# Score weights for the product with the values: 64x64 tiles, or 64x32 tiles four side by side

## The chip, the cores and the metric

The kernel runs on one core of a Trainium2 chip. The metric is the device time of one execution in microseconds (us); the time before is the median of three executions.

## What is computed

The reference has two stages. The first is a linear attention with decay, for 4 batches, 8 heads, 768 steps and a head width of 48. For each step t of each head,

```python
y[t] = r[t] @ (state + outer(u * k[t], v[t]))
state = w[t][:, None] * state + outer(k[t], v[t])
```

The second is a gated feed-forward layer on the result x of 3072 rows by 384: `(sigmoid(x @ w_gate) * (x @ w_val)) @ w_out`, with an inner width of 1536. All of it is in 32-bit floats.

## The kernel before

The attention is done by chunks of 128 steps: 6 chunks in each of 4 batches, 24 in all, numbered q. In the names, `pin` holds a chunk's decays, k and r with the head width on the partitions (two heads side by side, at partitions 0 to 47 and 64 to 111, so that p runs over 4 pairs of heads and o over the two of a pair); `tok` holds r, k and v with the steps on the partitions. A chunk is cut in two halves of 64 steps (`HALVES`), and goes through these functions:

- `prep_k`, `prep_r`, `fade` (lines 315 to 342) on VectorE (DVE) scale k, r and the state by running products of the decay.
- `turn_k` (352) transposes k on TensorE (PE), `take_k` copies it out on ScalarE (ACT), and `sums` (389 to 398) multiplies it with the values. Its weights are 64x64 for o = 0 and 64x48 for o = 1, and 48 value columns stream through. `middle` and `keep` (406, 410) update the state.
- `scores` (358 to 380) multiplies k and r to 64x64 blocks of scores (line 370, 48x64 weights, 64 columns stream) and r with the state into the result (line 377, 48x64 weights, 48 columns stream). The two heads and the two halves make four tiles of the array, used in turn.
- `mask` (383) copies the scores, with later steps set to zero, into the tile `at`, one DVE instruction for each o.
- `mix` (412 to 420) multiplies the masked scores, as weights, with the 48 columns of the values, and adds to the result. For half s the weights lie on the partitions of that half and the result goes to the partitions of the same half: the two tiles used are the two on the diagonal. The two heads of a pair write to two different PSUM banks, and `turn` swaps which half goes with which head. There are 2 x 4 x 2 = 16 calls in a chunk; in 32-bit floats each call is two weight loads and two products in the trace.
- `take_y` (424) on DVE adds the bonus term (made on GpSimd, POOL), `turn_x` (429) transposes the result on PE, and `take_x`, `rest_x` (438, 442) split it in a high and a low part.

The feed-forward layer works in groups of chunks of the four batches: `gate` and `value` (both line 450, tiles `pg` and `pu`, nine 128x128 products each), `sigmoid` and `hidden...` on ACT and DVE (461 to 476), `down` (485, tile `po`).

Two pieces of code set the order. Chunks 0 to 11, and the feed-forward groups that are ready by then, are ordered ahead of time by a planner (`Plan`, lines 141 to 187), which plays through costs written in the code; `mix` has a cost of 0.5 there (line 541), and the weights' own preparation (`w_...`, lines 242 to 266) is in the same plan. Chunks 12 to 23 follow a fixed pattern (`steps`, lines 583 to 603, and the loop at 607 to 625): each chunk's attention is spread over three feed-forward steps of the group before it. There `mix` comes right after a `gate`, and a `value` right after `mix`:

```python
gate(*a)
sigmoid(*a)
trio[i][0]()    # i == 1: mix, take_y twice, bonus1, bonus2 of the next chunk
value(*a)
```

Of the kernel before, what the change touches and what calls it, by code (L numbers as in the profile page):

```python
# [1 line left out]

# [16 lines left out]
B, H, S, D = 4, 8, 768, 48  # L19
# [5 lines left out]
NP = H // 2  # L25
# [12 lines left out]
HC = C // 2  # L38
HALVES = [slice(0, HC), slice(HC, C)]
# [151 lines left out]
def tile_kernel(ctx: ExitStack, tc: tile.TileContext, dec: bass.AP, tok: bass.AP, wts: bass.AP, u: bass.AP, out: bass.AP):  # L191
    nc = tc.nc
# [76 lines left out]
    pin, tk, eg, bon, kT, att, ready, mid, bank, x = {}, {}, {}, {}, {}, {}, {}, {}, {}, {}  # L269
# [115 lines left out]
    def values(q, p, o, half):  # L385
        h = 2 * p + o
        return tk[q][half, 2 * DM + h * D:2 * DM + (h + 1) * D]
# [24 lines left out]
    def mix(q):  # L412
        for turn in range(2):
            for p in range(NP):
                for s, half in enumerate(HALVES):
                    o = s ^ turn
                    nc.tensor.matmul(  # L417
                        bank["y", q, o][half, p], lhsT=att[q][half, o, p], rhs=values(q, p, o, half),
                        start=q < B and not s and p == 0, stop=p == NP - 1, skip_group_check=True,
                    )  # L420

    def take_y(q, o):
        mine = bon[q].rearrange("a (p o e) -> a o p e", o=2, e=D)[:, o]
# [91 lines left out]
    for q in range(3 * B + 2):  # L515
# [23 lines left out]
        add(f"m0{q}", "DVE", 0.42, [f"sc{q}"], k + 0.2, mask, q, 0)  # L539
        add(f"m1{q}", "DVE", 0.42, [f"m0{q}"], k + 0.2, mask, q, 1)  # L540
        add(f"mx{q}", "PE", 0.5, [f"m1{q}"], k + 0.3, mix, q, give=["at"])
        add(f"mid{q}done", None, 0, [f"sc{q}", f"keep{q}"], k, give=["mid"])
        add(f"y0{q}", "DVE", 0.36, [f"mx{q}", f"b4_{q}"], k + 0.3, take_y, q, 0, give=["bank"])
# [39 lines left out]
    def steps(q):  # L583

        def all_of(*todo):
            return lambda: [f(*a) for f, *a in todo]

        nxt = q + 1 < NG
        parts = [[[], [], []], [[], [], []], [[], [], []]]
        parts[0][0] += [(turn_k, q), (take_k, q)]  # L590
        parts[0][1] += [(sums, q), (middle, q)]
        if q < NG - B:
            parts[0][1] += [(keep, q)]
        parts[0][2] += [(scores, q), (mask, q, 0), (mask, q, 1)]
        parts[1][0] += [(mix, q), (take_y, q, 0), (take_y, q, 1)]
        parts[1][1] += [(turn_x, q), (take_x, q), (rest_x, q)]
        if q + 2 < NG:
            parts[1][1] += [(load, q + 2)]
        if nxt:
            parts[1][0] += [(bonus1, q + 1), (bonus2, q + 1)]  # L600
            parts[1][2] += [(prep_k, q + 1), (fade, q + 1)]
            parts[2][1] += [(bonus3, q + 1), (bonus4, q + 1), (prep_r, q + 1), (guard, q + 1)]
        return [[all_of(*todo) for todo in trio] for trio in parts]
# [57 lines left out]
```

## Time and profile before

| | |
|---|---|
| three executions | 620.81, 620.96, 621.43 us |
| the profiled execution | 622.11 us |
| its span, first to last instruction | 620.4 us |
| PE busy (products) | 577.6 us, 93% |
| PE weight loads busy | 513.6 us, 83% |
| DVE busy | 334.7 us, 54% |
| ACT busy | 201.5 us, 32% |
| POOL busy | 96.6 us, 16% |
| mean granted TensorE clock | 0.984 |

PE is the row of products on TensorE, PEld that of the weight loads, which can go on beside products. A busy share is over the whole span, so stretches with other limits are mixed in it. Records of products overlap: each has its latency in it, and the ends are modelled, so the distance between starts says more than a record's length. A granted clock of 1.0 is 2.4 GHz, and 0.5 is 1.2 GHz.

Of the rows further down: a busy-time row has the stretch and its length, the busy us (and instructions) of PE, PEld, DVE, ACT and POOL, then the granted clock, the DMA share and GB/s. With one line alone only the engines that it uses are there. A row of waits has the us in total, the times and the longest. A timeline row has the first start, the us from there to the last end, the engine, the line, what is written and read, rows*columns of the weights, the streamed operand, and the number of instructions. A row of groups ends with busy us, mean ns of one, and idle time before.

### The profile page before, as it was taken

Reading aid. Unit: us, or ns where it says so; the run is one execution under the profiler, and the core shown is the slowest. Engines: PE = TensorE matmul, PEld = TensorE weight load, DVE = VectorE, ACT = ScalarE, POOL = GpSimd, SP = SyncE. Lnnn points to the kernel's source line nnn. Section 1 sums busy time; section 2 is a strip of 40 time slices with the busy share of each in tenths; the row PEclk is TensorE's granted clock in tenths of the full one; section 3 lists DMA queues with packets and bytes.
Section 4 is the critical chain, followed back from the end, with each engine's and each line's share of the span. In section 5 each row is a group of like instructions: output and inputs, shape, how many; then the busy total and the mean of one; then the engine's idle time right before and its main releaser. Section 6 shows DMA issues by size and latency. Waiting matters only on the chain. (4 is left out here: it accounts for less than half of the span.)

```text
span 620.4 us, 13068 instructions
## 1 busy us (share of the span) xinstructions
PE 577.6 (93%) x5706; PEld 513.6 (83%) x5706; DVE 334.7 (54%) x570; ACT 201.5 (32%) x402; POOL 96.6 (16%) x86
## 2 busy tenths in 40 slices
PE   4477799999999999799999999999999999999994
PEld 3376699999999999688888888888888888888884
DVE  4979879989575743234544544644644544212120
ACT  2638783444323322212312322312322312221112
POOL 3342111111121402002202202202202201000000
PEclk9998899999999999989999999999999999999999
DMA  8687920023223130121022042022042000000001
GB/s 247 232 323 275 348 85 1 2 84 109 76 82 124 46 123 1 52 84 50 35 84 53 33 134 66 18 84 69 17 135 84 1 1 2 25 28 0 1 2 55
DMA packets 12050, 50.76 MB, mean 82 GB/s; under 512 B 1376, under 2 KB 4576, under 8 KB 10448
## 3 DMA queue, kind: packets, MB, share of 16 engines
q1 hardware_dynamic: 8528, 45.11, 22.2%
q10 hardware_dynamic: 3456, 4.72, 2.1%
q8 instruction: 47, 0.77, 0.5%
q14 instruction: 19, 0.16, 0.1%
HBM read 45.11 MB, written 4.72 MB: 80 GB/s over the span
## 5 line engine op out<-in xcount | busy, mean ns | idle before, releaser
L450 PE MATMUL pg<-x,w 128*128 128x256 f32 (+1 forms) x864 | 173.9, 347 | 1.2 <-DVE w L266 1.2
L450 PE MATMUL pu<-x,w 128*128 128x256 f32 (+1 forms) x864 | 171.4, 344 | 0.0
L450 PEld LDWEIGHTS pg<-x,w 128*128 128x128 f32 x864 | 137.9, 193 | 18.0 <-DVE w L266 1.6
L450 PEld LDWEIGHTS pu<-x,w 128*128 128x128 f32 x864 | 136.7, 192 | 17.2
L485 PE MATMUL po<-w,hh 128*128 128x384 f32 x576 | 147.8, 338 | 0.0
L468 DVE TENSOR_TENSOR sg<-pu,sg 128x256 f32<-128x256 f32 (+1 forms) x96 | 53.4, 556 | 151.2 <-PE pu L450 150.1
L485 PE MATMUL po<-w,hl 128*128 128x384 f32 x288 | 101.6, 353 | 7.2 <-DVE hl L476 7.0
L485 PEld LDWEIGHTS po<-w,hh 128*128 128x128 f32 x576 | 105.2, 189 | 0.9
L472 ACT CAST hh<-sg 128x256 fp32r<-128x256 f32 (+1 forms) x96 | 49.1, 512 | 168.9 <-DVE sg L468 168.4
L461 ACT ACTIVATE sg<-pg 128x256 f32<-128x256 f32 (+1 forms) x96 | 46.9, 488 | 158.9 <-PE pg L450 158.1
L313 POOL TENSOR_TENSOR bon<-tok,a 128x384 f32<-128x384 f32 x24 | 35.2, 1465 | 296.9 <-DVE a L309 296.9
L476 DVE TENSOR_TENSOR hl<-sg,hh 128x256 fp32r<-128x256 f32 (+1 forms) x96 | 55.1, 574 | 38.8 <-ACT hh L472 38.8
L485 PEld LDWEIGHTS po<-w,hl 128*128 128x128 f32 x288 | 54.4, 189 | 10.7 <-DVE hl L476 8.7
L302 POOL TENSOR_TENSOR bon<-tok,ub 128x384 f32<-128x384 f32 x24 | 31.9, 1330 | 117.5 <-DMA tok<-tok 51.1
L424 DVE TENSOR_TENSOR bon<-pa,bon 128x192 f32<-128x192 f32 x48 | 15.6, 352 | 42.3 <-PE pa L417 42.3
L347 ACT ACTIVATE junk<-eg 112x1032 bf16<-112x1032 f32 x24 | 25.6, 1066 | 31.2 <-DVE eg L337 31.1
L417 PEld LDWEIGHTS pa<-tok,at 64*64 64x64 f32 x768 | 26.7, 143 | 9.1 <-issue 5.1
L320 DVE TENSOR_TENSOR_SCAN eg<-pin,ends 112x516 f32<-112x516 f32 x24 | 30.0, 1249 | 4.2 <-DMA pin<-dec 4.2
L417 PE MATMUL pa<-tok,at 64*64 64x48 f32 x768 | 29.9, 229 | 2.3 <-DVE at L383 2.3
L383 DVE TENSOR_TENSOR at<-pa,after 128x256 f32<-128x256 f32 x48 | 18.6, 418 | 24.7 <-PE pa L377 24.7
L337 DVE TENSOR_TENSOR_SCAN eg<-pin,heads 112x516 f32<-112x516 f32 x24 | 31.0, 1292 | 0.0
L395 PEld LDWEIGHTS pv<-tok,kT 64*48 64x48 f32 (+1 forms) x704 | 21.0, 137 | 10.7 <-issue 4.7
(58 smaller groups left out, 445.1 us busy)
## 6 DMA issues: line engine op xcount, KB each, us to landing
pin<-dec SPq DMA_DIRECT2D x23, 675.5 KB, 5.1
tok<-tok SPq DMA_DIRECT2D x24, 576.0 KB, 4.3
wraw<-wts SPq DMA_DIRECT2D x12, 1152.0 KB, 12.1
y<-o ACTq DMA_DIRECT2D x24, 192.0 KB, 2.1
pin<-dec SPq DMA_DIRECT2D x1, 448.0 KB, 4.1
pin<-dec SPq DMA_DIRECT2D x1, 227.5 KB, 2.6
ub<-u SPq DMA_DIRECT2D x1, 192.0 KB, 7.4
```

Source lines behind the costliest of these rows:

```text
L302: nc.gpsimd.tensor_tensor(out=bon[q], in0=tk[q][:, 0:DM], in1=ub, op=ALU.mult)
L313: nc.gpsimd.tensor_tensor(out=by_head(bon[q]), in0=by_head(tk[q][:, 2 * DM:]), in1=a0, op=ALU.mult)
L320: nc.vector.tensor_tensor_scan(out=e[:, 516:0:-1], data0=t[:, 516:0:-1], data1=ends[:, 516:0:-1], initial=0.0, op0=ALU.mult, op1=ALU.add,)
L337: nc.vector.tensor_tensor_scan(out=e[:, WW:WW + 516], data0=t[:, 0:516], data1=heads[:, 0:516], initial=0.0, op0=ALU.mult, op1=ALU.add,)
L347: nc.scalar.activation(junk, both, AF.Square, accum_out=acc_d[:, q:q + 1])
L417: nc.tensor.matmul(bank["y", q, o][half, p], lhsT=att[q][half, o, p], rhs=values(q, p, o, half), start=q < B and not s and p == 0, stop=p ...
L450: nc.tensor.matmul(t, lhsT=w[f][:, cols], rhs=x[n][:, a, k, i0 * C:i1 * C], start=k == 0 and j == 0, stop=k == NKT - 1 and j == 2)
L461: nc.scalar.activation(sg, hid["g", n, f, i0], AF.Sigmoid)
L468: nc.vector.tensor_tensor(out=sg, in0=hid["u", n, f, i0], in1=sg, op=ALU.mult)
L472: nc.scalar.copy(hh, hid["s", n, f, i0])
L476: nc.vector.tensor_tensor(out=hl, in0=hid["s", n, f, i0], in1=hid["hi", n, f, i0].bitcast(F32), op=ALU.subtract)
L485: nc.tensor.matmul(po[n, i][:, :DM], lhsT=h[:, c], rhs=w[f][:, 2 * DM:], start=f == 0 and j == 0, stop=f == NFF - 1 and j == 2,)
```

## The change

In `mix`, the weights of a call are no longer the 64 columns of a half, but 32 of them, in a loop over i = 0 and 32 that stands between the loop over p and that over the halves. The output rows are cut the same way. So a chunk has 32 calls in place of 16, and four consecutive calls go to four tiles of 64x32: the first and third in the upper half of the array's rows, the second and fourth in the lower half. The values that stream are the same 48 columns, once for each call. The planner's costs are the same as before. The import at the top is used nowhere in the lines shown.

```diff
+import heapq
 from contextlib import ExitStack
...
     def mix(q):
         for turn in range(2):
             for p in range(NP):
-                for s, half in enumerate(HALVES):
-                    o = s ^ turn
-                    nc.tensor.matmul(
-                        bank["y", q, o][half, p], lhsT=att[q][half, o, p], rhs=values(q, p, o, half),
-                        start=q < B and not s and p == 0, stop=p == NP - 1, skip_group_check=True,
-                    )
+                for i in range(0, HC, 32):
+                    for s, half in enumerate(HALVES):
+                        o = s ^ turn
+                        some = slice(half.start + i, half.start + i + 32)
+                        nc.tensor.matmul(
+                            bank["y", q, o][some, p], lhsT=att[q][half, o, p, i:i + 32], rhs=values(q, p, o, half),
+                            start=q < B and not s and p == 0, stop=p == NP - 1, skip_group_check=True,
+                        )
```

## Rows read from the trace of the kernel before

**Rows 1.** Busy time of all engines by stretch.

```profile
0.00:80.00 80.00, 51.91 (x648) 46.17 (x649) 63.46 (x89) 47.76 (x84) 23.59 (x30) 0.94 0.77 277
80.00:257.00 177.00, 172.92 (x2072) 165.30 (x2071) 121.91 (x223) 65.47 (x149) 30.01 (x26) 1.00 0.22 67
257.00:535.00 278.00, 276.24 (x2622) 235.26 (x2621) 131.96 (x229) 69.92 (x138) 42.98 (x31) 0.99 0.18 54
```

**Rows 2.** What PE waited for, 80 to 257 us, then 257 to 535.

```profile
PE po L485 <- DVE hl L476: 3.0, 3, 1.5
PE pk L352 <- DVE pin L326: 0.6, 1, 0.6
PE pk L352 <- DVE mid L406: 0.2, 1, 0.2
PE pk L352 <- PE pg L450: 0.2, 1, 0.2
...
PE pa L370 <- DVE mid L406: 1.6, 1, 1.6
```

**Rows 3.** Busy time by stretch of line 417 alone (PE, PEld).

```profile
0.00:80.00 80.00, 6.96 (x128) 6.18 (x128) 0.94 0.77 277
80.00:257.00 177.00, 9.08 (x256) 8.09 (x256) 1.00 0.22 67
257.00:535.00 278.00, 13.90 (x384) 12.41 (x384) 0.99 0.18 54
```

**Rows 4.** Timeline of PE around the mix of chunk 13.

```profile
291.84 0.39 PE L450 MATMUL pg<-x,w 128*128 128x512 f32 x1
292.16 1.13 PE L417 MATMUL pa<-tok,at 64*64 64x48 f32 x32
293.22 0.50 PE L450 MATMUL pu<-x,w 128*128 128x512 f32 x1
```

**Rows 5.** Line 417 from 290 to 300 us: lengths of one, min/median/max.

```profile
L417 PEld LDWEIGHTS pa<-tok,at x32: 129/135/135, 292.2 to 293.0; 64*64 64x64 f32 x32
L417 PE MATMUL pa<-tok,at x32: 218/218/253, 292.2 to 293.1; 64*64 64x48 f32 x32
```

**Rows 6.** Timeline of PE, a sums block with one half only (chunk 20).

```profile
447.26 0.66 PE L395 MATMUL pv<-tok,kT 64*64 64x48 f32 x16
```

**Rows 7.** Groups by form, 447.25 to 447.61 us (first two rows) and to 447.62.

```profile
L395 PE MATMUL pv<-tok,kT 64*64 64x48 f32 x6 | 0.5, 224 | 0.0
L395 PE MATMUL pv<-tok,kT 64*48 64x48 f32 x7 | 0.5, 210 | 0.0
...
L395 PE MATMUL pv<-tok,kT 64*48 64x48 f32 x8 | 0.6, 209 | 0.0
```

**Rows 8.** Timeline of PE: transposes with 112 and 128 streamed columns.

```profile
283.08 0.55 PE L352 MATMUL pk<-ident,pin 112*128 112x112 f32 x4
...
295.41 0.49 PE L429 MATMUL px<-ident,bon 128*128 128x128 f32 x3
```

**Rows 9.** Lengths of these transposes (lines 352 and 429, one chunk each).

```profile
L352 PE MATMUL pk<-ident,pin x4: 257/258/259, 283.1 to 283.4; 112*128 112x112 f32 x4
...
L429 PE MATMUL px<-ident,bon x3: 272/273/273, 295.4 to 295.6; 128*128 128x128 f32 x3
```

**Rows 10.** Timeline of PE, the scores of chunk 13 and what follows.

```profile
288.81 0.70 PE L370 MATMUL pa<-pin 48*64 48x64 f32 x32
289.33 0.21 PE L377 MATMUL pa<-ready,pin 48*64 48x48 f32 x2
289.34 0.21 PE L377 MATMUL pa<-mid,pin 48*64 48x48 f32 x2
...
289.72 0.23 PE L377 MATMUL pa<-ready,pin 48*64 48x48 f32 x2
289.74 0.22 PE L377 MATMUL pa<-mid,pin 48*64 48x48 f32 x2
289.89 2.33 PE L450 MATMUL pg<-x,w 128*128 128x512 f32 x9
```

**Rows 11.** Busy time, scores to mix: chunk 12, and chunk 13.

```profile
262.32:270.15 7.83, 7.69 (x106) 6.08 (x106) 1.11 (x3) 0.60 (x1) 0.00 (x0) 0.56 0.33 88
288.81:293.22 4.41, 4.41 (x106) 3.65 (x105) 0.75 (x2) 0.60 (x1) 0.00 (x0) 1.00 0.46 127
```

**Rows 12.** What DVE waited for from PE's line 417, 0 to 80 us.

```profile
DVE bon L424 <- PE pa L417: 0.8, 1, 0.8
```

**Rows 13.** The page's totals and instruction queue; PE's waits, 0 to 80 us.

```profile
PE 577.6 (93%) x5706; PEld 513.6 (83%) x5706; DVE 334.7 (54%) x570; ACT 201.5 (32%) x402; POOL 96.6 (16%) x86
...
q8 instruction: 47, 0.77, 0.5%
...
PE pk L352 <- issue: 2.5, 1, 2.5
```

**Rows 14.** Timeline of PE before the clock fell: the longest waits.

```profile
250.10 0.44 PE L485 MATMUL po<-w,hl 128*128 128x384 f32 x1 [1.20 <-DVE hl L476]
...
253.96 0.45 PE L485 MATMUL po<-w,hl 128*128 128x384 f32 x1 [1.48 <-DVE hl L476]
...
262.32 1.48 PE L370 MATMUL pa<-pin 48*64 48x64 f32 x29 [1.62 <-DVE mid L406]
```

## The prediction

> **What bounds the kernel now.** I read the busy time by stretch first. Up to 80 us PE is busy 52 of 80 and DVE 63; from 80 to 257 us PE is busy 173 of 177, and from 257 to 535 it is busy 276 of 278, with DVE at two thirds of the first and under half of the second [rows 1]. Then the waits: after 80 us all that PE still waits for is some 4 us before 257 and 1.6 us after it [rows 2]. The waits of 3.0 and 1.6 us are for DVE steps (the low part of the hidden values, the middle state) that PE's own products feed, so they move with PE. So after 80 us a microsecond less of PE time in the middle of its queue is a microsecond off the end; before that DVE leads.
>
> Next, where the touched line runs. It has 128, 256 and 384 products in the three stretches [rows 3]; at 32 a chunk that is 4, 8 and 12 blocks. So 20 of the 24 blocks lie where PE is the bound.
>
> Then one such block. It begins at 292.16 and the next load is at 293.22 [rows 4]: 1.06 us with nothing else on PE. The group lasts 1.13 us to its last end, and one product's record is 0.218 [rows 5], so from first to last start there are 0.91 us, and 0.15 us of drain follow before the array takes 128x128 weights. Thirty-two products in 0.91 us is 29 ns each. The products alternate between two diagonal tiles, so the block is 16 rounds of two. The sums block [rows 6] has one 64x64 tile with 8 products: 0.66 - 0.22 = 0.44 us from first to last, 7 gaps. With a rhythm R and a start-up e: 15R + e = 0.91 and 7R + e = 0.44 give R = 58 ns and e = 35 ns. One tile takes a product each 58 ns; two tiles do so side by side.
>
> **The change, part by part.** It removes 16 rounds of two products with 64-column weights in each block, and puts in 16 rounds of four with 32-column weights. Products and loads double, from 32 to 64 each, so 768 more of each in the run. No wait, copy or DMA issue is added; the masks are waited for at the same places, the first products on either bank.
>
> *The round.* No row has a 32-column load, so I bound R. In the sums block the 64x48 tile runs beside the 64x64 one and streams the same 48 columns. Seven of its products have started by 447.61 and eight by 447.62, against six of the other [rows 7]; its eight starts lie within 0.35 us, so 7R + e = 0.35 and R = 45 ns. Sixteen columns less in the load took 13 ns off. Upper end for a tile by itself: 45 ns, as the 32-column load is shorter still and the stream the same. Lower end: 13 ns less again, 32 ns, if the load alone sets the rhythm. Which of them depends on how long 48 values take to stream. The transposes tell: four with 112 streamed columns are (0.55 - 0.258)/3 = 97 ns apart, three with 128 are (0.49 - 0.273)/2 = 108 ns apart, with 128-column weights in both [rows 8, 9]. That is about 0.86 ns a streamed column, so 48 need some 41 ns, and with the few ns that each product carries besides, 45. I take 45: the stream, not the load, is then the limit, and the last third of the load's cut is lost. The Trainium skill ("TensorE: Matmul & The Clock Gate", Back-to-back issue gap) gives N/2.4 + 2.5 ns for N streamed columns; for 48 that is 22 ns, and the round would fall to the load's 32. The transposes here took twice its price a column.
>
> *Four tiles at once.* R = 45 needs a product each 11 ns. In the scores, four 64-column tiles start 32 products from 289.33 to 289.74 [rows 10], one in 13 ns on average. So the rate is a little beyond what the trace shows sustained. I take it that four tiles keep their own rhythms, as the two sums tiles of unlike width do [rows 7]; the ends of this are the second and third rival below.
>
> *The block.* First to last start: 35 + 15 x 45 ns, and 0.02 for the offsets of the four tiles (four starts lie within 0.02 us at 289.33 [rows 10]): 0.73 us; 0.91 before, so 0.18 less. The drain: the record of a product is 0.224 us with 64 columns and 0.210 with 48 in the same window [rows 7], 13 ns for 16 columns, so 27 ns less with 32 if the drain follows it; ends 0 and 0.03, I take 0.03 since a tile then has half the columns. Sum 0.21 us a block.
>
> *The total.* 20 x 0.21 = 4.2 us. One of the 20, in chunk 12, runs partly at half clock [rows 11]; it is counted like the others. The four early blocks count nothing: DVE is their cover, and it waited for line 417 only once, 0.8 us [rows 12]; were that cover gone, they would give 4 x 0.21 = 0.8 us more.
>
> *What else is issued.* 1536 instructions more in PE's queue. The instruction queue now brings 47 packets for the program, and PE waited for issue once, 2.5 us, before 80 us [rows 13]. An eighth more on PE, which now has 5706 loads and 5706 products, means about 6 packets more, at 0.5% of 16 x 620 us / 47 = 1.1 us each. I cost them at nothing: the loads of `gate` and `value`, 2 us on either side of a block, cover a fetch; without cover it is 6 us.
>
> *The sum.* The profiled execution took 622.11 us with a span of 620.4; less 4.2 it is 617.9. It stands 1.15 above the median of 620.96; the same step down from the median gives **616.8**.
>
> **The rivals.**
>
> *The load alone sets the rhythm* (R = 32). Then 35 + 15 x 32 + 20 = 0.53 us, 0.41 less a block with the drain, 8.2 in all: 612.8. For it: the 13 ns step between 48 and 64 columns at one and the same stream. Against it: the transposes. Chance 0.11.
>
> *Nothing comes of it.* Either a 32-column load in a tile takes what a 64-column one takes, so that the change does not do what it says, or four tiles cannot go faster than in the scores. At R = 58 the block is 0.93, +0.01 with no gain in the drain: 621.2. At one product in 13 ns it is 63 x 13.2 = 0.83, 0.08 less: 619.3. For it: no row is faster than the 13 ns. Against it: in the scores the 64-column load already explains 58 ns a round, so their pace needs no other limit. Chance 0.18, a sixth of it at the 619.3 end.
>
> *Two tiles in one quarter take turns* (the other side). The first and third call of a round lie in the same 64x64 quarter of the array. The trace has tiles side by side only in different quarters. If the two must follow each other, a round is 2 x 45 = 90 ns, the block 35 + 15 x 90 + 20 = 1.4 us, 0.49 more: 20 x 0.49 = 9.8, so 630.8. It decides as soon as a round is over 57 ns, (0.91 - 0.055)/15. Against it: the two sums tiles share the rows of a half and do not hinder each other [rows 7]. Chance 0.11.
>
> *A floor for each product.* If the 29 ns between products in the mix were a floor for any product, 63 x 29 = 1.83 us, 0.92 more a block: 639. The scores' 13 ns speak against it [rows 10]. Chance 0.02. The Trainium skill ("TensorEngine Tiling (Array Packing)", Instruction Overhead) has such a floor, about 60 cycles a product, and warns against taking tiles from a dimension that is small already; at 2.4 GHz that is 25 ns, an estimate of 63 x 25 = 1.6 us and some 634 in all. The trace does not agree, with its 13 ns.
>
> *The clock.* From the scores to the mix chunk 12 took 7.83 us at a mean granted clock of 0.56, much of it at 1.2 GHz, and chunk 13 took 4.41 at 2.4 GHz [rows 11]. Before it fell PE had waited for DVE three times within 14 us, 1.2, 1.5 and 1.6 us [rows 14]. With PE 1.7 us earlier there, that stretch may not come (3.4 less: 613.4; chance 0.07), or a second one may (3.4 more: 620.2; chance 0.05). The three executions lie within 0.6 us, so it hardly varies by itself.
>
> **How the numbers follow.** Forecast 0.46, rivals as given; together 1. A measurement of this kernel can tell about 0.2%, 1.2 us, from no change. Faster by more: forecast, load alone, the stretch that goes, and the 619.3 end: 0.46 + 0.11 + 0.07 + 0.03 = 0.67. Within: 0.15 of nothing and 0.05 of the second stretch, 0.20. Slower: 0.11 + 0.02 = 0.13. The range goes from the load alone (612.8, a little below for an early gain of 0.3) to 621.5, nothing gained and 0.3 of scatter; it leaves out the slower cases, 0.13. The forecast's own range is 616.0 (with the early 0.8) to 618 (20 blocks of 0.15, a pace between 11 and 13 ns).
>
> **What would show it.** Line 417 with 1536 products, 64x32 weights, loads some 27 ns shorter than 135, and lengths near 191. A block's distance from its first load to that of `pu` near 0.85 us, against 1.06 [rows 4]. PE's busy time about 5 us lower, DVE's unchanged, the chunks' period in the second half 0.2 us shorter. Wrong: a block at 0.65 (load alone), at 1.06 or 0.95 (nothing), or above 1.1 (turns); or waits of PE that grow by what the block lost.

## The result and the profile after

The changed kernel takes 613.38 us (median of four executions, 611.23 to 616.97) against 620.88 before. The ratio is 0.9894, with a 95% interval of 0.9868 to 0.992: 5.0 to 8.2 us less. That is faster than the forecast of 616.8 and its own range of 616.0 to 618, and inside the whole range. The changed executions lie 6 us apart, and the profiled one is the slowest of the four, so the trace has to be read by stretches and not by its end.

The page's totals after, beside [rows 13]:

```profile
PE 572.2 (93%) x6474; PEld 508.6 (83%) x6474; DVE 334.5 (54%) x570; ACT 201.6 (33%) x402; POOL 95.6 (16%) x86
...
q8 instruction: 53, 0.87, 0.6%
```

PE has 768 products and 768 loads more and is busy 5.4 us less. DVE, ACT and POOL have the instructions that they had. The instruction queue brings 53 packets in place of 47, as reckoned.

The block of chunk 13 in the timeline of PE, beside [rows 4], and its records, beside [rows 5]:

```profile
289.19 0.61 PE L453 MATMUL pg<-x,w 128*128 128x512 f32 x2
289.73 0.89 PE L420 MATMUL pa<-tok,at 64*32 64x48 f32 x64
290.55 0.50 PE L453 MATMUL pu<-x,w 128*128 128x512 f32 x1
```

```profile
L420 PEld LDWEIGHTS pa<-tok,at x64: 103/107/107, 289.7 to 290.4; 64*32 64x32 f32 x64
L420 PE MATMUL pa<-tok,at x64: 202/203/228, 289.7 to 290.4; 64*32 64x48 f32 x64
```

From the first load to the next one of `pu` it is 0.82 us, 1.06 before: 0.25 less by the unrounded starts. From first to last start it is 0.89 - 0.20 = 0.69, and with the start-up of 0.035 and 0.02 of offsets, 15R = 0.63: a round of four now takes 42 ns, a round of two took 58. The drain is 0.13, it was 0.15.

By stretch, beside [rows 1] (the last one ends at 530 here):

```profile
0.00:80.00 80.00, 51.16 (x740) 45.46 (x742) 62.31 (x87) 45.66 (x81) 21.79 (x29) 0.89 0.81 277
80.00:257.00 177.00, 173.40 (x2375) 165.84 (x2371) 122.98 (x225) 68.02 (x153) 30.84 (x26) 1.00 0.22 69
257.00:530.00 273.00, 271.24 (x3001) 230.55 (x3001) 131.94 (x229) 69.55 (x138) 43.01 (x31) 0.99 0.18 54
```

PE is as full after 80 us as it was. In the first stretch its granted clock is 0.89, where it was 0.94: in this execution a half-clock stretch more fell there.

### The profile page after: what moved, and what is told of

The parts are those of the page before. It is cut to its first block, busy times and chain, and to the rows that moved or that the text cites. A ratio compares the mean times of both kernels' runs of the same rounds, so it can differ in the third digit from the quotient of the medians.

```text
span 615.3 us, 14604 instructions
## 1 busy us (share of the span) xinstructions
PE 572.2 (93%) x6474; PEld 508.6 (83%) x6474; DVE 334.5 (54%) x570; ACT 201.6 (33%) x402; POOL 95.6 (16%) x86
## 5 line engine op out<-in xcount | busy, mean ns | idle before, releaser
L306 POOL TENSOR_TENSOR bon<-bon,tok 128x384 f32<-128x384 f32 x24 | 27.7, 1153 | 1.7
L353 PE MATMUL pk<-ident,pin 112*128 112x112 f32 x96 | 14.6, 278 | 14.0 <-DVE pin L327 10.2
```

Of the source, the lines that this page charges most:

```text
L306: nc.gpsimd.tensor_tensor(out=bon[q], in0=bon[q], in1=tk[q][:, DM:2 * DM], op=ALU.mult)
```

## The experiments

There were eleven runs, three of them of the two kernels as they are. Three questions stood: what sets the round of 42 ns, whether the four tiles or the narrow loads make the gain, and where the rest of the 7.5 us comes from, as 20 blocks of 0.25 are 5.0.

### What sets the round: only 24 of the 48 value columns

```diff
+        width = D if q < B else D // 2
...
-                            bank["y", q, o][some, p], lhsT=att[q][half, o, p, i:i + 32], rhs=values(q, p, o, half),
+                            bank["y", q, o][some, p, :width], lhsT=att[q][half, o, p, i:i + 32], rhs=values(q, p, o, half)[:, :width],
```

> The changed kernel with only the first 24 of the 48 value columns multiplied in chunks 4 to 23; the other 24 columns of each head are left without this product. Theory A (the stream of 48 columns sets the round of 42 ns): the round falls until the 32-column load sets it, to about 32 ns, and the block from 0.81 to 0.63 to 0.67 us; 20 blocks give some 3 us. Rival C (instructions are delivered to the array at one product in 10.6 ns): the round stays at 42 ns and the block at 0.81 us. Rival D (the load of 32 columns takes 42 ns): the same as C.

Measured: 608.37 us in one execution. The timeline of PE and, under it, how many products had started 0.08 and 0.24 us after the block's first (groups by form, 282.43 to 282.52, then to 282.68):

```profile
282.44 0.74 PE L421 MATMUL pa<-tok,at 64*32 64x24 f32 x64
283.11 0.50 PE L454 MATMUL pu<-x,w 128*128 128x512 f32 x1
```

```profile
L421 PE MATMUL pa<-tok,at 64*32 64x24 f32 x8 | 0.3, 196 | 0.0
...
L421 PE MATMUL pa<-tok,at 64*32 64x24 f32 x28 | 0.4, 189 | 0.0
```

The block is 0.67 us, at the upper end of what A expected. Between the two counts 20 products started in 0.16 us, one in 8 ns: a round of 32 ns, the price of a 32-column load by the 13 ns step of [rows 7]. Over the whole block, with records of 0.186 us, it is (0.74 - 0.19 - 0.055)/15 = 33. So neither the load (D) nor the delivery of instructions (C) was at its limit at 42 ns; the stream of 48 columns was, or something else that goes with the number of columns, such as writing them, which this cut does not tell apart. What sets the 32 ns is not shown by it either: the load's price fits.

### The order: two tiles at a time

```diff
-        for turn in range(2):
-            for p in range(NP):
-                for i in range(0, HC, 32):
+        for i in range(0, HC, 32):
+            for turn in range(2):
+                for p in range(NP):
```

> The changed kernel with the loop over i outermost: the same 64 products of a chunk, but first all those of the tiles at columns 0 and 64, then all those of the other two. Theory A (a tile takes a product each 42 ns; the gain is that four tiles do so side by side): 32 rounds of two, about 0.035 + 31 x 0.042 = 1.35 us from first to last, a block of 1.45 to 1.5 us, 0.4 us more than the 1.06 of the kernel before; 20 blocks give some 8 us more than before, a ratio of 1.010 to 1.015. Rival (narrow loads are cheaper in any order, or the array takes products at one rate for all tiles): a block as in the changed kernel, 0.81 us, a ratio of 0.99.

Measured: 626.74 us, ratio 1.0111 (1.008 to 1.0143): slower than before by 5 to 9 us.

```profile
291.32 1.42 PE L420 MATMUL pa<-tok,at 64*32 64x48 f32 x64
292.66 0.51 PE L453 MATMUL pu<-x,w 128*128 128x512 f32 x1
```

The same 64 products and loads, 0.82 us with four tiles in turn, take 1.34 us here. Narrow loads by themselves lose; the gain is theirs only together with the second pair of tiles. The block is 0.1 us shorter than A's 1.45: from first to last start it has 1.22 us, where 31 rounds of 42 ns would take 1.3. The counts of products started 0.53 and 0.67 us after the first one (groups by form, 291.31 to 291.85, then to 291.99) show why:

```profile
L420 PE MATMUL pa<-tok,at 64*32 64x48 f32 x24 | 0.7, 205 | 0.0
...
L420 PE MATMUL pa<-tok,at 64*32 64x48 f32 x38 | 0.9, 205 | 0.0
```

The first 24 are twelve rounds of two; with the start-up of 35 ns, that puts the round between 41 and 45 ns. In the next 0.14 us there are 14, where two tiles at 42 ns start 6 or 7: the second pair starts before the first has ended. So a tile has the same 42 ns with one neighbour at work as with three.

### The two parts of the kernel, and the changed kernel again

`late_only` and `early_only` take the width from the chunk:

```diff
+        step = 32 if q >= 3 * B else HC
...
-                for i in range(0, HC, 32):
+                for i in range(0, HC, step):
```

(`early_only` has `q < 3 * B`.) `again` and `again2` are the changed kernel without an edit, in two sessions.

> The changed kernel once more. Theory A: each block is 0.25 us shorter, which is 5.0 us over the 20 blocks where PE is the bound, and what the median gained beyond that (7.5 in all) is a half-clock stretch that is shorter or missing; then the executions scatter by 2 to 6 us, spans go with the mean clock (a lower clock, a longer span), and a profile with a clock of 0.986 or more has a span of 609 to 612 us and blocks of 0.81 us as in the slower profile. Theory B: the early stage starts PE sooner, so the 2.5 us are there at equal clock: a profile with the clock of before (0.984) would still lie near 612 to 613, and the first block after 80 us would start 2 us sooner than before.

> 32-column weights only in chunks 12 to 23, 64-column ones before. Theory A: nothing changes ahead of the first of these chunks, so the half-clock stretches near 58 and 262 us stay as they were before, and the gain is 12 x 0.25 = 3.0 us: a median of 617.6 to 618.2, with little scatter. A rival by which the clock falls or rises with the weights' width itself: a stretch more or less among the late chunks, 3 us or more off that.

> 32-column weights only in chunks 0 to 11. Theory A: 8 blocks after 80 us give 2.0 us, and the earlier arrival at the end of the planned stage changes the half-clock stretch there: a median of 616 to 617 (4 to 5 us less than before), with a scatter as in the changed kernel and a mean clock that differs between executions. Theory B: the same median with the clock as before. If the two parts do not add up to the 7.5 us of the whole, the rest lies in how they meet at the change of stages.

> The changed kernel a third time, beside the same runs of the kernel before. Theory A: between 612 and 615, and a difference to the kernel before that lies between 5 and 7 us, as the stretches fall. Theory H: 7 us again or more.

| | median (lowest to highest) | ratio to before (interval) |
|---|---|---|
| again | 613.39 (610.42 to 614.46) | 0.9893 (0.9862 to 0.9924) |
| again2 | 613.91 (609.87 to 617.43) | 0.9894 (0.9856 to 0.9931) |
| late_only | 616.68 (614.77 to 618.09) | 0.9943 (0.9923 to 0.9963) |
| early_only | 617.70 (612.75 to 619.38) | 0.9942 (0.9916 to 0.9968) |

The kernel before was at 620.23 (617.33 to 622.70, 23 executions) beside the first three of these, so it too lies over 5 us wide. The parts, 3.5 and 2.5 us, add up to 6.1, near the whole, 6.8, within its interval. But neither came where A put it: `late_only` was to be at 617.6 or more with little scatter, and is at 616.7 with 3 us of it. `early_only` has no middle: five executions at 612.8 to 614.6 with mean clocks of 0.988 to 0.991, seven at 617.5 to 619.4 with 0.980 to 0.988. So most of the steps of 3 to 5 us within one kernel go with the clock, though not all: at 0.988 there is 613.9 and 617.5. `again2` has them as well: three executions near 610 at a clock of 0.991, four at 613.8 to 616.2 and 617.4 at 0.980 to 0.983. Its median is where A put it, 6.6 us under the kernel before beside it (620.48).

For `again` neither theory came whole. Its profile has a clock of 0.983 and took 613.4 us; that of the kernel before took 622.1 at 0.984. That is close to what B expected, 612 to 613 at the clock of before. But the mix of chunk 4 starts at 83.19, 1.0 us sooner than the 84.18 of before, and not 2 as B had it.

### The clock: the kernel before again, and the wait at the change of stages

`before_again` is the kernel before. `no_gap` is the changed kernel with this, and `before_no_gap` the kernel before with the same:

```diff
                 value(*a)
+                begins = n == 2 and not j and not i
+                if begins:
+                    trio[i][1]()
                 hidden(*a)
                 hidden_hi(*a)
                 hidden_lo(*a)
-                trio[i][1]()
+                if not begins:
+                    trio[i][1]()
```

> The kernel before once more, for a second profile of it. Theory A (a block costs 1.065 us always, and the half-clock stretches vary by themselves from execution to execution): from the mix of chunk 12 to that of chunk 23 it takes 253 us as before, while the time up to the mix of chunk 4 (84.2 us) and from there to chunk 12 (184.6) differ by 1 to 3 us, with the length of the half-clock stretches near 60 and 262 us. Rival E (the longer stretch at 262 us belongs to the kernel before and the change shortens it): the stretch is 6.8 us again, and 184.6 us again from chunk 4 to chunk 12.

> The changed kernel with another order at the change of stages alone: in the first step of the fixed pattern the sums and the middle state are put ahead of the hidden values, so that the scores wait less for DVE (1.6 us now). Theory F (that wait brings the half-clock stretch near 262 us): the wait falls to about 0.5 us, 1.1 us less, and the stretch goes in most executions, another 1.7 us: a median 2 to 3 us under the changed kernel. Rival G (the stretch comes from the waits of 1.2 and 1.5 us ahead of it as well): 1.1 us less, and the stretch still there in the profile.

> The kernel before, with the order at the change of stages of no_gap. With the half-clock stretch near 262 us out of both, the difference to no_gap (611.1) is the change alone. Theory A (20 blocks of 0.25 us, and what the medians differed by beyond that is scatter of the stretches): 616.1, between 615.5 and 617. Theory H (the change gives 1.5 to 2.5 us more than its blocks, in the early stage or by the clock): 617.5 to 618.5.

`before_again` took 620.08 us in one execution. The busy time of all engines by two stretches, the third number from the right being the granted clock: the kernel before, `before_again`, the changed kernel, `again2`, and `no_gap`:

```profile
55.00:80.00 25.00, 18.83 (x221) 16.79 (x218) 22.46 (x33) 19.02 (x35) 4.93 (x4) 0.80 0.86 332
255.00:272.00 17.00, 15.24 (x169) 12.12 (x168) 3.39 (x8) 2.99 (x6) 0.00 (x0) 0.80 0.26 74
```

```profile
55.00:80.00 25.00, 18.89 (x209) 16.98 (x210) 22.47 (x34) 19.01 (x36) 4.70 (x5) 0.80 0.86 328
255.00:272.00 17.00, 15.24 (x179) 12.56 (x178) 4.42 (x10) 3.55 (x8) 0.00 (x0) 0.90 0.32 100
```

```profile
55.00:80.00 25.00, 18.73 (x211) 17.00 (x208) 21.07 (x31) 16.79 (x32) 3.97 (x3) 0.66 0.94 338
255.00:272.00 17.00, 15.24 (x212) 12.39 (x212) 4.52 (x10) 3.78 (x8) 0.00 (x0) 0.90 0.31 100
```

```profile
55.00:80.00 25.00, 19.47 (x298) 17.47 (x299) 21.41 (x33) 19.48 (x34) 4.86 (x4) 0.86 0.81 302
255.00:272.00 17.00, 15.90 (x194) 13.70 (x195) 8.36 (x17) 2.92 (x6) 0.00 (x0) 1.00 0.25 76
```

```profile
55.00:80.00 25.00, 19.54 (x238) 17.68 (x239) 20.93 (x30) 17.85 (x33) 2.75 (x2) 0.73 0.89 324
255.00:272.00 17.00, 16.68 (x224) 13.87 (x223) 7.84 (x16) 3.30 (x7) 0.00 (x0) 1.00 0.25 77
```

The first two are one kernel, and its time at 1.2 GHz in the second stretch is half as long in the one as in the other. The third and fourth are one kernel too, and in the fourth none is left. So the half-clock time comes and goes by itself with the wait of 1.6 us standing, and rival E falls. `two_at_a_time` too has that wait, and a clock of 1.00 in the second stretch.

With the wait taken out, `no_gap` is at 611.09 (610.52 to 613.31), ratio 0.9857 (0.9832 to 0.9882), 2.3 us under `again`, which ran in another session, as F expected, though the intervals of the two ratios overlap; its wait is 0.2 us, and the stretch is absent. `before_no_gap` has none either. That fits F, that the wait brings the stretch where it comes, though the two waits ahead of it still stood and one profile of each kernel is little.

`before_no_gap` is at 616.98 (615.51 to 619.61), ratio 0.9936 (0.9915 to 0.9957). To `no_gap` that is 5.9 us: within A's 615.5 to 617, and short of H's 617.5. But the clock was not like in the two: its executions had 0.989 on average, those of `no_gap` 0.986. At 0.986 to 0.988 alone the medians are 617.3 (five) and 610.8 (four), 6.5 apart, so H is not excluded. As both traces are free of half-clock time between 80 us and the end of the products, they can be laid beside each other. The starts of the mix of chunks 4, 12 and 23, `before_no_gap` and then `no_gap`:

```profile
86.01 1.14 PE L417 MATMUL pa<-tok,at 64*64 64x48 f32 x32
...
266.38 0.32 PE L417 MATMUL pa<-tok,at 64*64 64x48 f32 x4
...
519.33 0.38 PE L417 MATMUL pa<-tok,at 64*64 64x48 f32 x6
```

```profile
84.05 0.89 PE L420 MATMUL pa<-tok,at 64*32 64x48 f32 x64
...
261.62 0.37 PE L420 MATMUL pa<-tok,at 64*32 64x48 f32 x16
...
511.86 0.33 PE L420 MATMUL pa<-tok,at 64*32 64x48 f32 x12
```

From chunk 4 to 12 it is 180.37 and 177.57 us, 2.8 less; from 12 to 23 it is 252.95 and 250.24, 2.7 less; and from there to the ends of the spans, 617.9 and 609.9, 98.6 and 98.0, some 0.5 less. In all 6.0. The blocks are 8, 11 and 1 times 0.25: 2.0, 2.75 and 0.25. The fixed pattern has nothing but them; the planned stage has 0.8 more. PE's waits from 80 to 262 us, again `before_no_gap` and `no_gap`, hold most of it:

```profile
PE po L485 <- DVE hl L476: 2.9, 3, 1.5
PE pk L352 <- DVE pin L326: 0.7, 1, 0.7
PE pk L352 <- DVE mid L406: 0.2, 1, 0.2
```

```profile
PE po L488 <- DVE hl L479: 2.7, 2, 1.5
PE pk L353 <- DVE pin L327: 0.6, 1, 0.6
PE pa L371 <- DVE mid L407: 0.2, 1, 0.2
```

The last row of the second is at the change of stages, and `before_no_gap` has the same one just after 262. So 3.8 us of waits became 3.3: the short waits of the planned stage got shorter or went. That this is the change's doing is not shown. `late_only` has the old weights up to chunk 11, and its waits from 80 to 265 us are, to the tenth, those of the changed kernel in `again2`:

```profile
PE po L489 <- DVE hl L480: 2.7, 2, 1.5
PE pa L371 <- DVE mid L407: 1.6, 1, 1.6
PE pk L353 <- DVE pin L327: 0.6, 1, 0.6
```

So these short waits come and go with the old weights alone. From chunk 4 to 12, each with a clock of 0.90 from 255 to 272 us, `before_again` and `late_only` take 183.1 and 182.2 us, the changed kernel and `again` 180.5 both: 1.7 to 2.6 less, about the 2.0 of the blocks. From chunk 12 to 23 no such doubt is left: it is 252.9 to 253.2 us in the four profiles with 64-column weights there (`before`, `before_again`, `before_no_gap`, `early_only`) and 250.2 in the five with 32 columns and no other change of the blocks (the changed kernel, `again`, `again2`, `late_only`, `no_gap`).

### Four tiles in the sums as well, and the best of it

```diff
+        for p in range(NP):
+            for s, half in halves:
                 for o, m in ((0, 64), (1, D)):
```

> The changed kernel with the sums of the two halves interleaved, so that four tiles (two of 64x64, two of 64x48) are in use at once in place of two and then two. Theory A (each tile keeps its own rhythm, 58 and 45 ns): from first to last product 0.094 + 6 x 0.058 + 0.02 = 0.46 us in place of 0.72, 0.26 less in a chunk that has both halves; 16 such chunks lie where PE is the bound, 4.2 us less than the changed kernel: a ratio to the kernel before of 0.981 to 0.985. Rival (tiles in the same columns of the array hinder each other): 0.72 as now and a ratio of 0.989.

> The changed kernel with the interleaved sums and with the order of no_gap. Their gains were 2.3 us each on the changed kernel, one on sums blocks, the other on a wait and a half-clock stretch: if they add, 608.5 to 609.5, a ratio of 0.981 to 0.983; if the stretch was what both gained, 611 as each alone.

`sums4`: 611.13 (609.42 to 611.33), ratio 0.985 (0.9826 to 0.9873). The two timeline rows of its sums, and the scores behind them:

```profile
277.91 0.67 PE L399 MATMUL pv<-tok,kT 64*64 64x48 f32 x32
278.51 0.45 PE L491 MATMUL po<-w,hl 128*128 128x384 f32 x1
...
280.82 0.74 PE L371 MATMUL pa<-pin 48*64 48x64 f32 x29
...
282.01 1.20 PE L456 MATMUL pg<-x,w 128*128 128x512 f32 x4
```

The sums block is 0.60 us from its start to the next products, against 0.87 for two tiles and then two, as A expected. But against `again` the median is 2.3 us less, and not 4.2. The scores that follow take 1.19 us where they took 1.08 [rows 10], in the chunks 13 to 19; that is 0.8 of the missing 1.9, and the rest is open. In `again` the update of `state` (`keep`, on DVE) ended 0.2 us ahead of the first load of the scores, in `sums4` 0.07 after it:

```profile
282.58 0.36 DVE L411 TENSOR_TENSOR state<-pv,mid 112x192 f32<-112x192 f32 x1
283.14 0.38 PEld L371 LDWEIGHTS pa<-pin 48*64 48x64 f32 x20 [0.25 <-DVE state L411]
...
280.53 0.36 DVE L414 TENSOR_TENSOR state<-pv,mid 112x192 f32<-112x192 f32 x1
280.82 0.61 PEld L371 LDWEIGHTS pa<-pin 48*64 48x64 f32 x29 [0.25 <-issue]
```

So PE now comes to the scores before DVE is through, and I read the longer block as a wait for DVE inside it.

`both`: 608.37 (606.79 to 608.80), ratio 0.9801 (0.9767 to 0.9835), just under 608.5 to 609.5: the two gains add. It beats the changed kernel of the same session (`again2`) by 5.5 us.

## Why the prediction was right, and where it was off

**What bounds the kernel** held. In the fixed pattern eleven blocks less 0.25 us each gave 2.7 us, the full sum.

**The round** was the right term, with a size a little off: 45 ns was taken, 42 measured. The reason given was the right one. The stream of 48 columns is the limit, at the transposes' price of 0.86 ns a column, 41 ns; what was added to it "besides" is 1 ns and not 4. That the transposes were the row to price it by was not argued, and in that there was luck: the nine 512-column products of `gate`, whose tiles are float32r in the kernel, start (2.33 - 0.39)/8 = 0.24 us apart [rows 4, 10], some 0.47 ns a column, and by that price the load would have set the round. The round of 32 ns with the cut stream agrees with the lower bound taken for the load. On the Trainium skill's N/2.4 + 2.5 ns ("TensorE: Matmul & The Clock Gate", Back-to-back issue gap): 22 ns for 48 columns, an estimate, would have let the load set 32, and so would the 25 ns that the section's table has for up to 64 columns; measured were 42.

**Four tiles at once** go at one product in 11 ns, faster than any row of before, and with 24 columns in 8.

**The drain** lost 0.016 us and not 0.03. It does follow the records: they fell by 15 ns, from 218 to 203, where 27 were taken and lengths near 191 forecast. Both together make 0.25 a block, where 0.21 was predicted: 5.0 us and not 4.2.

**The waits.** Of PE's waits for DVE it was said that they move with PE. The pair of profiles without half-clock time has 0.8 us beyond the blocks in the planned stage, 0.5 of it in shorter waits, and 0.25 beyond the block at the end. But `late_only` shows the shorter waits with the old weights, so the runs do not show a term that was left out here.

**The clock** was a rival of 0.12, and "it hardly varies by itself" is the sentence that failed. Three executions within 0.6 us had been too few: the kernel before ranges over 5 us in 23, with half-clock stretches that differ between two profiles of it. That the measured 613.38 falls on the 613.4 of the stretch that goes, and near the 612.8 of the load alone, is chance: the block is 0.82 us and not 0.65, and the stretch is there in the first profile of the changed kernel.

**What the blocks do not cover.** The blocks give 5.0 us. The kernel before averages 620.5 us over the 53 executions beside `again`, `no_gap` and `again2`, the changed kernel 613.4 over its 18, with mean clocks of 0.985 and 0.986: 7.1 us less, and not by the mean clock. At 0.991 alone it is 616.0 to 617.6 (three) against 609.9 to 611.0 (four). So the change seems to bring some 2 us more than its blocks, and no run places them. The four early blocks, which the prediction counted as nothing, are a candidate; the traces cannot tell, as the mix of chunk 4 starts between 81.0 and 86.4 us in the changed kernel's three profiles, and between 83.7 and 86.0 in the three with the old weights throughout.

**The other rivals.** *Turns in one quarter* fell: a round of 42 ns is shorter than the 57 from which it would have decided, with two tiles in each quarter. *A floor of 29 ns a product* fell with 11 ns, and with it the Trainium skill's some 60 cycles a product ("TensorEngine Tiling (Array Packing)", Instruction Overhead), an estimate of 25 ns at 2.4 GHz: across tiles it does not hold here. *Nothing comes of it* fell on both its grounds. *The load alone* fell with the round of 42 ns; the cut to 24 columns came to the 32 ns that it expected.

## What to carry to other kernels

Price a small 32-bit product by tile: here the rhythm of one tile was the longer of its load and its stream, each about 0.85 ns a column plus a few ns, and tiles in different places ran side by side. The price is that of these operands; the float32r products of `gate` are cheaper by the column. So keep all the tiles that the shapes allow in turn, and cut the weights only until the load is under the stream (a further cut was not tried): with the order wrong, the same cut cost 6.5 us. And take the scatter of the kernel before from many executions ahead of reading a gain of one per cent: compare stretches, and executions, at the same granted clock.

## What was not expected of the hardware

Products did not all start in the order of the program: in `two_at_a_time` those of the second pair of tiles began while the first pair still had some to start. Two profiles of one and the same program differ by half in the time spent at 1.2 GHz near 262 us, behind the same waits. And behind a sums block that ends sooner the scores took 0.11 us longer.
